# First token groups in a written order, token sets halved when made, two weight buffers, in an FNet plus ReGLU kernel

## The chip, the cores and the metric

The kernel runs on one core of a Trainium2 chip. The metric is the device time of one execution in microseconds (us): the median of 3 runs is 1048.98 us before the change (1047.89 to 1051.33). Engines are TensorE (PE, matrix products), VectorE (DVE), ScalarE (ACT), GpSimd (POOL) and SyncE (SP, which issues most loads).

## The reference

```python
# x [1, 2048, 640]; dft_seq [2048, 2048]; dft_hid [640, 640]
# W_gate, W_up [640, 1728]; W_down [1728, 640], all float32
def _A_ref(x, dft_seq_re, dft_seq_im, dft_hid_re, dft_hid_im):
    a = jnp.einsum("bsd,ed->bse", x, dft_hid_re)
    b = jnp.einsum("bsd,ed->bse", x, dft_hid_im)
    return jnp.einsum("ts,bse->bte", dft_seq_re, a) - jnp.einsum("ts,bse->bte", dft_seq_im, b)

def _B_ref(x, W_gate, W_up, W_down):
    gate = jnp.einsum("bsd,df->bsf", x, W_gate)
    up = jnp.einsum("bsd,df->bsf", x, W_up)
    gate = gate * (gate > 0)
    return jnp.einsum("bsf,fd->bsd", gate * up, W_down)

xn = _layernorm(x, axis=-1)          # (x - mean) / sqrt(var + 1e-5), no scale or shift
return x + _A_ref(xn, ...) + _B_ref(xn, ...)
```

## The kernel before

**Splitting.** Every product is made to float32 accuracy from a reduced format: an operand is split into a high part (the copy rounded to the format, on ACT) and a low part (operand minus high, on DVE), and `mm3` (L126) issues three matmuls for a block: high by high (L129), high by low of the moving operand (L130), low by high (L131). `split` (L122) makes both parts: ACT at L123, then DVE at L124. Large matrix products are made of 2 by 2 blocks in seven products instead of eight, so sums and differences of blocks have to be split too. A matmul takes 128 by 128 weights and 512 moving columns.

**Phase 1, the sequence transform (to about 411 us).** The 2048 tokens are 8 groups of 256 (`SG` = 2 tiles of 128; `NH` = 4 groups in each half). The output columns come in 4 chunks of 512. In chunks 0 and 1 the streams `B11` and `B21` go straight over groups 0 to 7 (`first_stream`, L506), chunk by chunk in turn (`B1100 B1110 B1101 B1111 ...`: name, chunk, group); after that each chunk pair runs over `T1`, `T2`, `B22`, `T3`, `T4` with four blocks each (`stream`, L593; T10 is the first block of T1). A unit of work has a load, a preparation, a run and a finish; `drive(4, 2)` (L677) issues the load of unit i, the preparation two units later and the run four units later. Raw blocks of the transform's matrix lie in the pool `raw` (6 tiles), split blocks in a ring of 3 (`cb`), so the preparation of a block waits for the third block before it on PE.

**The layer norm** runs along with the first stream. `layernorm(g)` (L236) takes statistics on DVE (`ln_stats`, L200), the root with ACT and small DVE instructions (`ln_root`, L206), centers and scales one tile on DVE and one on ACT, makes the high part on ACT and the low part on DVE (L251). Groups 0 to 3 go to `xs_early`, groups 4 to 7 to `xs_late`. Group 0 has its own written order, `first_group` (L284), in which POOL makes the lows of the first two raw blocks in four pieces of 512 columns (L291). Group 1 has `second_group` (L263). `first_products` (L474) and `second_products` (L448) give the matmuls of groups 0 and 1 in an order of their own. `keep_in_program_order` and `issue_after` are hints to the scheduling layer that sets the order on the engines; `pin` applies the first to a list.

**Token sets.** The second and third phase work on the transposed tokens. `token_sets(q, step)` (L320) makes, in six steps for each half q of the tokens, nine blocks of 128 by 1024: five plain ones or sums (`B11, B12, B21, B22, X4`) and four sums (`T1` to `T4`). It loads rows of the transposed x and of the statistics, normalizes (`make`), forms sums (`more`) on DVE and writes the float32 result to memory (`sets`). The steps for q = 1 are placed within phase 1, nine units apart: steps 2 to 5 run in chunks 1 and 2. In chunk 3, `load_set` (L661, units `K` and `A` of L727) loads each of the nine sets through a `stage` tile and splits it on ACT and DVE into its place in `xs_early` (A) or `sets_b` (K).

**Phase 2 (`gate_up`, L786, 26 units, to about 745 us).** Unit n needs the weights of column block n: `Weights(n)` loads 128 by 1280 into the one buffer of pool `z` (L748, L750), `sums` forms differences, `high` copies (L766) and `low` subtracts (L770) into `gw`. While unit n computes, the weights of n + 1 are split, and after that `Weights(n + 2)` is loaded (L822). The copy `p1` at L812 reads the first product out of PSUM. `lead_load` (L947) fetches the first block for phase 3.

**Phase 3 (`project`)** multiplies by the transform over the hidden dimension and by the down weights, and adds x.

Of the kernel before, what the change touches and what calls it, by code (L numbers as in the profile page):

```python
# [58 lines left out]
def fnet_reglu_kernel(  # L59
# [34 lines left out]
    sets = [dram_p.tile([NSET, P, W2], F32, name=f"set{q}") for q in range(2)]  # L94
# [141 lines left out]
    def layernorm(g):  # L236
# [17 lines left out]
        if g == 2:  # L254
            with tc.issue_after(high.ins), tc.issue_after(low.ins):
                st = stage()[:, :CH].rearrange("p (j d) -> p j d", j=SG)
                for j in range(SG):
                    nc.scalar.activation(st[:, j], ln_place(0)[:, j, K2], AF.Copy, scale=stat[:, 1, 0, j : j + 1])
                keep_a21(0, st)
# [3 lines left out]
    def second_group():  # L263

        xs, bs, mv = ln_tiles(1)
        js = slice(0, SG)
        nm, r = (stat[:, i, 1, js] for i in range(2))
        with tc.issue_after(late["ln"]):
            for i in ln_stats(1, xs, bs, mv, js):
                pass  # L270
            for i in ln_root(1, mv, js):
                tc.keep_in_program_order(i)
            nmr = mv[:, js, 6]
            late["ln"] = tc.keep_in_program_order(nc.vector.tensor_tensor(nmr, nm, r, op=OP.mult)).ins
            highs = [nc.scalar.activation(xn_block(1, K14, 0)[:, j], xs[:, j, K14], AF.Identity,
                                          bias=mv[:, j, 6:7], scale=stat[:, 1, 1, j : j + 1]) for j in range(SG)]
            for j in range(SG):
                nc.vector.tensor_scalar(xs[:, j], xs[:, j], mv[:, j, 0:1], stat[:, 1, 1, j : j + 1],
                                        op0=OP.subtract, op1=OP.mult)
            low = nc.vector.tensor_tensor(xn_block(1, K14, 1), xs[:, :, K14], xn_block(1, K14, 0).bitcast(F32), op=OP.subtract)  # L280
            keep_a21(1)
        late["first"] = [i.ins for i in highs + [low]]

    def first_group(b):  # L284


        pin = lambda steps: [tc.keep_in_program_order(i) for i in steps]
        xs, bs, mv = ln_tiles(0)
        part = lambda c, j: b[c][1][:, j * CH : (j + 1) * CH]
        high = lambda c, j: [nc.scalar.activation(b[c][0][:, 0, j], part(c, j), AF.Copy)]  # L290
        low = lambda c, j: [nc.gpsimd.tensor_tensor(b[c][0][:, 1, j], part(c, j), b[c][0][:, 0, j].bitcast(F32),  # L291
                                                    op=OP.subtract)]
        j0, j1 = slice(0, 1), slice(1, 2)
        d0, d14, rest, every = slice(0, P), slice(P, 3 * P), slice(P, D), slice(0, D)
# [4 lines left out]
        pin([nc.gpsimd.tensor_tensor(mv[:, 0, 6:7], stat[:, 1, 0, 0:1], stat[:, 1, 0, 0:1], op=OP.mult)])  # L299
# [12 lines left out]
        pin(ln_stats(0, xs, bs, mv, j1))  # L312
        pin(ln_root(0, mv, j1))
        pin(ln_center(0, xs, mv, 1, every, nc.scalar))
        pin(ln_scale(0, xs, 1, d0))
        pin(ln_scale(0, xs, 1, d14))
        pin(high(1, 1))
        late["ln"] = pin(low(1, 1))[-1].ins

    def token_sets(q, step, stage=stage, unit=None):  # L320
# [6 lines left out]

        def later(load, make, keep):
            def begin():
                load()  # L330
                for m in make:
                    defer(6, m)
                defer(8, keep)

            todo.append((begin, idle, idle, idle))

        unit = unit or later

        if step < 2:
# [12 lines left out]
            unit(load, [make], lambda: nc.gpsimd.dma_start(sets[q][X4][:, cs], t["a"]))  # L352
            return

        k, hs = (step - 2) // 2, (step - 2) % 2 * HC
        hs = slice(hs, hs + HC)
        cols = lambda ap: ap.rearrange("p (c t) -> p c t", c=2)

        def load():
            t["mr"], t["ab"] = stage(), stage()  # L360
            for i in range(2):
                nc.gpsimd.dma_start(cols(part(t["mr"], i)), cols(st_r[i : i + 1])[:, :, hs].to_broadcast([P, 2, HC]))
                nc.gpsimd.dma_start(cols(part(t["ab"], i)), cols(ch[k + 2 * i])[:, :, hs])

        def make():
            mr, ab = t["mr"], t["ab"]
            for i in range(2):
                tc.keep_in_program_order(tt(part(ab, i), part(ab, i), part(mr, 0), op=OP.add))
                tt(part(ab, i), part(ab, i), part(mr, 1), op=OP.mult)

        def more():

            mr, ab = t["mr"], t["ab"]
            (a0, a1, b0, b1), (t1, t2, t3, t4) = ([st[:, i * HC : (i + 1) * HC] for i in range(4)] for st in (ab, mr))
            sub = lambda o, i0, i1: tt(o, i0, i1, op=OP.subtract)
            sub(t1, a1, a0)
            sub(t2, b1, t1)
            sub(t3, b1, a1)
            sub(t4, b0, t2)

        def keep_sets():
            cs = slice(k * CH + hs.start, k * CH + hs.stop)
            for i, st in ((B11, t["ab"]), (T1, t["mr"])):
                nc.gpsimd.dma_start(sets[q][i : i + 4, :, cs].rearrange("i p t -> p i t"),
                                  st.rearrange("p (i t) -> p i t", i=4))

        unit(load, [make, more], keep_sets)
# [60 lines left out]
    def second_products(b):  # L448

        keys = [("e1", 0), ("e1", 1), "v1"]  # L450
        for js, vs in (((0,), (0, 2)), ((1,), (0, 2)), ((0, 1), (1,))):
            for j in js:
                for v in vs:
                    for d, key in zip((0, 1, 4), keys):
                        nc.tensor.matmul(E[0, key], xn_part(SG + j, d)[v == 1], b[:, int(v == 2), j], start=False, stop=False)
# [18 lines left out]
    def first_products(j, b):  # L474

        keys = [("e1", 0), ("e1", 1), "v1"]
        for v, cs in (((0, (0,)), (1, (0,)), (2, (0,)), (0, (1,)), (1, (1,)), (2, (1,))),
                      ((0, (0,)), (2, (0,)), (0, (1,)), (1, (0,)), (2, (1,)), (1, (1,))))[j]:
            for c in cs:
                for d, key in zip((0, 1, 4), keys):  # L480
                    if j == 0 and v == 0:
                        E[c, key] = bank()
                    nc.tensor.matmul(E[c, key], xn_part(j, d)[v == 1], b[c][0][:, int(v == 2), j],  # L483
                                     start=j == 0 and v == 0, stop=False)
# [21 lines left out]
    def first_stream(c, name, g):  # L506
# [7 lines left out]
        def load():  # L514
            if n == 0 and c == 0:
                st = start["raw"] = [raw(), raw()]
                for j in range(SG):
                    ln_load(0, slice(j, j + 1))
                    for k in range(2):
                        i = (k + j) % 2  # L520
                        nc.sync.dma_start(st[i][:, j * CH : (j + 1) * CH], dft[i, 0, 0][:, j * CH : (j + 1) * CH])
# [3 lines left out]
            if n > 0 or c > 1:  # L525
                t["s"] = raw()
                nc.sync.dma_start(t["s"], dft[c, 0, n])

        def prepare():
# [4 lines left out]
            if norm is not None:  # L534
                (second_group if norm == 1 else lambda: layernorm(norm))()
            if n > 0 or c > 1:
                t["b"] = b = parts()

                with ExitStack() as order:
                    for i in late["first"] if (c, n) == (1, 1) else ():  # L540
                        order.enter_context(tc.issue_after(i))
                    split(flat(b, 0), flat(b, 1), t["s"])

        def run():
# [3 lines left out]
            if n == 1 and c == 0:  # L548
                second_products(t["b"])
                return  # L550
            accs = [(c, ("e1", i)) for i in range(2)]
            product(g, t["b"], resident(n, 0), accs, half == 0, half == 1, ((c, "v1"), half, half == 0))
# [96 lines left out]

    def set_parts(q, i):  # L650
        if i in SETS_A:
            t, b = xs_early, (SETS_A_NEXT, SETS_A)[q].index(i) * 2 * W2
        else:
            t, b = late["sets_b"][q], SETS_B.index(i) * 2 * W2
# [6 lines left out]
    def load_set(q, blocks, get=stage):  # L661
        t = {}
# [12 lines left out]
        return load, prepare, idle, idle  # L675
# [21 lines left out]
    def phase(c, names):  # L697


        for n in names.split():  # L700
            if n == "K":
                todo.append(load_set(1, [first_sets.pop(0)]))
            elif n == "A":
                todo.append(load_set(1, [early_sets.pop(0)]))
# [545 lines left out]
```

## Time and profile before

| What | Value |
|---|---|
| median of 3 runs | 1048.98 us |
| span of the profiled execution, first to last instruction | 1043.3 us |
| PE busy | 1028.4 us (99%) |
| DVE busy | 802.1 us (77%) |
| ACT busy | 433.5 us (42%) |
| POOL busy | 95.7 us (9%) |
| matmuls | 4528, of which 48 warm up |
| mean granted PE clock | 0.997 |

The profile is of one execution, and of that one only the span is known, not a time of its own beside the runs; the three runs lie 4.6 to 8.0 us above the span, their median 5.7.

How to read what follows. A line of the timeline has the start, the duration, the engine, the line of the program, the operation, output <- inputs, shape and count, and in brackets the idle time of the engine just before it with what ended it. "L124 DVE cb<-raw,cb" is thus the low part of a transform block. In a list of waits stand the total, the number of times and the longest. A line of windows begins with the stretch and its length, then for each engine busy us and (xcount), then the granted clock of PE, the share of DMA engines at work and the rate in GB/s. A matmul is shown with 0.39 us but starts 0.227 us after the one before.

### The profile page before, as it was taken

The numbers are of one execution on the slowest core, as the hardware profiler recorded it, in microseconds if no ns is written. First come the engines' busy times: TensorE is split into PE (matmuls) and PEld (weight loads), VectorE is DVE, ScalarE is ACT, GpSimd is POOL, SyncE is SP. The second block draws the span as 40 slices with busy tenths as digits, with TensorE's granted clock in tenths as the row PEclk, the third lists the DMA queues.
The fourth block names the chain that finished last, engine by engine and source line by source line (L and its number), as shares of the span: only waits on it lengthen the run. The fifth ranks groups of instructions, "written<-read, shape, count | busy, mean of one in ns | idle before, by whom it ended". The sixth has DMA issues, their size and how long they took to land.

```text
span 1043.3 us, 12416 instructions
## 1 busy us (share of the span) xinstructions
PE 1028.4 (99%) x4528; PEld 847.3 (81%) x4528; DVE 802.1 (77%) x1071; ACT 433.5 (42%) x543; POOL 95.7 (9%) x156
## 2 busy tenths in 40 slices
PE   8999999999999899899999999999999999999998
PEld 7888888888887788688888888888888888888886
DVE  7857886978979887577887988887488667786764
ACT  6654453333333443333334534343355423552521
POOL 2000010101211001421110000100000000000000
PEclk9999999999999999999999999999999999999999
DMA  7985754958867863863364566565498637986454
GB/s 294 340 247 170 261 161 140 311 205 269 305 199 259 339 203 116 251 222 143 131 206 177 203 224 232 215 237 188 145 393 287 207 111 218 366 300 233 157 159 121
DMA packets 100156, 233.29 MB, mean 224 GB/s; under 512 B 11392, under 2 KB 50816, under 8 KB 98688
## 3 DMA queue, kind: packets, MB, share of 16 engines
q1 hardware_dynamic: 83664, 166.96, 47.6%
q0 software_dynamic: 16432, 65.55, 17.4%
q8 instruction: 35, 0.57, 0.2%
q14 instruction: 25, 0.20, 0.1%
HBM read 177.41 MB, written 54.02 MB: 222 GB/s over the span
## 4 chain that ended last, share of the span: by engine, by line
PE 84%; DMA 5%; DVE 5%; issue 4%; ACT 2%; POOL 0%; SPq 0%; ACTq 0%; POOLq 0%; DVEq 0%
PE ps L131 27%; PE ps L130 27%; PE ps L129 27%; DMA z<-in_wgu 2%; DVE cb L124 1%; DMA r<-in_x 1%; DMA st<-set 1%; PE ps L1147 1%; PE ps L483 1%; ACT cb L123 1%; DMA set<-st 1%; DMA rw<-hd 1%; DVE raw L595 0%; DVE gw L770 0%; ACT gw L120 0%
## 5 line engine op out<-in xcount | busy, mean ns | idle before, releaser
L131 PE MATMUL ps<-cb,wt 128*128 128x512 f32 x390 | 151.9, 390 | 0.1
L129 PE MATMUL ps<-cb,wt 128*128 128x512 f32 x390 | 151.8, 389 | 0.0
L130 PE MATMUL ps<-cb,wt 128*128 128x512 f32 x390 | 151.7, 389 | 0.0
L124 DVE TENSOR_TENSOR cb<-rw,cb 128x1024 fp32r<-128x1024 f32 x83 | 94.2, 1135 | 66.6 <-ACT cb L123 65.9
L123 ACT ACTIVATE cb<-rw 128x1024 fp32r<-128x1024 f32 x83 | 81.9, 987 | 145.2 <-PE ps L131 125.0
L123 ACT ACTIVATE cb<-raw 128x1024 fp32r<-128x1024 f32 x78 | 82.5, 1059 | 124.9 <-PE ps L131 108.3
L124 DVE TENSOR_TENSOR cb<-raw,cb 128x1024 fp32r<-128x1024 f32 x78 | 95.1, 1221 | 41.2 <-ACT cb L123 38.0
L130 PE MATMUL ps<-xs_early,gw 128*128 128x512 f32 x260 | 101.2, 389 | 0.0
L129 PE MATMUL ps<-xs_early,gw 128*128 128x512 f32 x260 | 101.2, 389 | 0.0
L131 PE MATMUL ps<-xs_early,gw 128*128 128x512 f32 x260 | 101.1, 389 | 0.0
L130 PE MATMUL ps<-cb,xs_late 128*128 128x512 f32 x256 | 99.8, 390 | 0.9 <-DVE cb L124 0.8
L131 PE MATMUL ps<-cb,xs_late 128*128 128x512 f32 x256 | 99.7, 389 | 0.3 <-DVE xs_late L251 0.3
L129 PE MATMUL ps<-cb,xs_late 128*128 128x512 f32 x256 | 99.6, 390 | 0.4 <-ACT cb L123 0.4
L130 PE MATMUL ps<-cb,xs_early 128*128 128x512 f32 x238 | 92.8, 390 | 1.5 <-DVE cb L124 1.5
L129 PE MATMUL ps<-cb,xs_early 128*128 128x512 f32 x238 | 92.6, 391 | 1.1 <-ACT cb L123 1.1
L120 ACT ACTIVATE gw<-z 128x1024 fp32r<-128x1024 f32 (+1 forms) x52 | 57.8, 1111 | 84.2 <-DVE z L760 68.7
L131 PE MATMUL ps<-cb,xs_early 128*128 128x512 f32 x238 | 92.1, 389 | 0.0
L131 PEld LDWEIGHTS ps<-cb,wt 128*128 128x128 f32 x390 | 73.2, 188 | 15.7 <-DVE wt L124 0.5
L130 PEld LDWEIGHTS ps<-cb,wt 128*128 128x128 f32 x390 | 73.2, 188 | 15.4
L129 PEld LDWEIGHTS ps<-cb,wt 128*128 128x128 f32 x390 | 73.2, 188 | 15.2
L120 ACT ACTIVATE u<-ps 128x512 f32<-128x512 f32 x52 | 31.2, 599 | 93.0 <-PE ps L131 93.0
L770 DVE TENSOR_TENSOR gw<-z,gw 128x1024 fp32r<-128x1024 f32 (+1 forms) x52 | 64.8, 1286 | 2.3 <-ACT gw L120 2.2
(192 smaller groups left out, 1932.1 us busy)
## 6 DMA issues: line engine op xcount, KB each, us to landing
raw<-in_dft SPq DMA_DIRECT2D x94, 512.0 KB, 5.7
wt<-wparts SPq DMA_DIRECT2D x66, 256.0 KB, 3.2
z<-in_wgu SPq DMA_DIRECT2D x26, 640.0 KB, 4.0
hd<-ob POOLq DMA_DIRECT2D x26, 512.0 KB, 3.5
rw<-hd SPq DMA_DIRECT2D x24, 512.0 KB, 6.1
wparts<-pw POOLq DMA_DIRECT2D x11, 1024.0 KB, 4.1
tk<-in_dft SPq DMA_DIRECT2D x16, 512.0 KB, 6.2
rw<-pq SPq DMA_DIRECT2D x16, 512.0 KB, 7.7
```

The source lines that it names most:

```text
L120: return nc.scalar.activation(o, i, AF.Copy)
L123: nc.scalar.activation(hi, src, AF.Copy)
L124: return nc.vector.tensor_tensor(lo, src, hi.bitcast(F32), op=OP.subtract)
L129: nc.tensor.matmul(ps, wh, mh, start=first, stop=False, skip_group_check=more)
L130: nc.tensor.matmul(ps, wh, ml, start=False, stop=False, skip_group_check=more)
L131: nc.tensor.matmul(ps, wl, mh, start=False, stop=last, skip_group_check=more)
L483: nc.tensor.matmul(E[c, key], xn_part(j, d)[v == 1], b[c][0][:, int(v == 2), j], start=j == 0 and v == 0, stop=False)
L770: tt(self.w[:, 1, cs], self.z[:, cs], self.w[:, 0, cs].bitcast(F32), op=OP.subtract)
L1147: nc.tensor.matmul(B[key], wr[:, v, es], hr[:, cs], start=False, stop=v == 1, skip_group_check=not new)
```

## The change

1. **Start.** `first_group` is rewritten: loads come as token tile 0, raw block of chunk 0 (first half), token tile 1, then the other raw halves; POOL's lows are placed behind a DVE result (`behind_vector`, a one-element POOL instruction that reads it), and DVE makes one of the four. `second_group` becomes `next_group`, which pins the order of groups 1 to 3; for groups 2 and 3, POOL makes the low of chunk 0's raw block in two pieces, for group 1 DVE does. `next_products` orders the matmuls of groups 1 to 3 of chunk 0, with the tokens' low part last.
2. **Token sets of q = 1.** `halve` splits each result when it is made, in one of eight places of a work area, and both halves are written to memory (`halves`, twice the bytes). In chunk 3 `load_halves` loads 128 by 2048 straight into place; its units `K` and `A` stand later in the list. Sets of q = 0 are stored whole as before, and `next_set` loads and splits them as before.
3. **Weights.** Pool `z` has two buffers; `Weights(n + 2)` is loaded at the beginning of `gate_up(n)`.
4. `lead_load` is ordered behind the last weights' load, `rest_weights` behind the last transform block.

```diff
+    def behind_vector(src):
+        src = src.bitcast(F32)
+        pin([nc.gpsimd.tensor_tensor(root_t, src, src, op=OP.mult)])
+
+    def next_group(g, b, raw, before):
+        xs, bs, mv = ln_tiles(g)
+        js = slice(0, SG)
+        nm, r = (stat[:, i, g, js] for i in range(2))
+        nmr = mv[:, js, 6]
+        low = lambda engine, j: pin([engine.tensor_tensor(flat(b, 1)[:, j], raw[:, j], flat(b, 0)[:, j].bitcast(F32), op=OP.subtract)])
+        pin(ln_stats(g, xs, bs, mv, js))
+        pin([nc.scalar.activation(flat(b, 0), raw, AF.Copy)])
+        if before is not None:
+            behind_vector(before)
+            for j in range(SG):
+                low(nc.gpsimd, slice(j * CH, (j + 1) * CH))
+        pin(ln_root(g, mv, js))
+        pin([nc.vector.tensor_tensor(nmr, nm, r, op=OP.mult)])
+        pin(nc.scalar.activation(xn_block(g, K14, 0)[:, j], xs[:, j, K14], AF.Identity,
+                                 bias=mv[:, j, 6:7], scale=stat[:, 1, g, j : j + 1]) for j in range(SG))
+        if before is None:
+            low(nc.vector, slice(0, W2))
+        pin(nc.vector.tensor_scalar(xs[:, j], xs[:, j], mv[:, j, 0:1], stat[:, 1, g, j : j + 1],
+                                    op0=OP.subtract, op1=OP.mult) for j in range(SG))
+        late["ln"] = pin([nc.vector.tensor_tensor(xn_block(g, K14, 1), xs[:, :, K14], xn_block(g, K14, 0).bitcast(F32),
+                                                  op=OP.subtract)])[0].ins
+        keep_a21(g)
...
     def first_group(b):
...
-        pin(high(0, 0))
-        pin(low(0, 0))
+        high(0, 0)
         h0, h14 = ln_scale(0, xs, 0, d0), ln_scale(0, xs, 0, d14)
         pin([next(h0)])
         pin(ln_center(0, xs, mv, 0, rest, nc.vector))
         pin([next(h14)])
-        pin(high(1, 0))
-        pin(low(1, 0))
+        high(1, 0)
         pin(h0)
         pin(h14)
-        pin(high(0, 1))
-        pin(low(0, 1))
+        behind_vector(places(0)[1][:, 3 * P - 1 : 3 * P])
+        low(0, 0, nc.gpsimd)
...
+        high(0, 1)
...
+        low(1, 0, nc.vector)
...
+        high(1, 1)
+        pin([nc.vector.tensor_tensor(l[:, K14], whole, h[:, K14].bitcast(F32), op=OP.subtract)])
+        behind_vector(l[:, 3 * P - 1 : 3 * P])
+        low(0, 1, nc.gpsimd)
+        low(1, 1, nc.gpsimd)
...
+        def begin():
+            load()
+            for i, (make, name, place, view) in enumerate(made):
+                def halve(make=make, name=name):
+                    for m in make:
+                        m()
+                    src = t[name]
+                    t["h" + name] = h = work()[:, : src.shape[1]]
+                    split(h.bitcast(F32R), src.bitcast(F32R), src)
+
+                def keep(name=name, place=place, view=view):
+                    for v, part in enumerate((t["h" + name], t[name])):
+                        nc.gpsimd.dma_start(place(v), view(part))
+
+                defer(6 + i, halve)
+                defer(8 + i, keep)
...
+    def load_halves(i):
         def load():
             if "sets_b" not in late:
                 late["sets_b"] = {1: get_r1(F32R)}
-            for i in blocks:
-                t[i] = get()
-                nc.sync.dma_start(t[i], sets[q][i])
-
-        def prepare():
-            for i in blocks:
-                split(*set_parts(q, i), t[i])
+            t, b = set_place(1, i)
+            with tc.issue_after(late["dma"]):
+                nc.sync.dma_start(t[:, b : b + 2 * W2].bitcast(F32), halves[i].rearrange("p v t -> p (v t)"))
...
-    phase(NCHUNK - 1, "T10 K T11 T12 K T13 T20 B220 K T21 B221 K T22 T23 B222 B223 T30 A T31 A T32 A T33 A T40 A T41 T42 T43")
+    phase(NCHUNK - 1, "T10 T11 T12 T13 T20 B220 T21 B221 T22 T23 K K K A A B222 B223 T30 A T31 A T32 A T33 T40 T41 T42 T43 K")
...
-    for n, b, side in (("prep", 2, "left"), ("z", 1, "left"), ("wr", 1, "left"), ("tmp", 1, "left"), ("hob", 2, "left"),
+    for n, b, side in (("prep", 2, "left"), ("tmp", 1, "left"), ("wr", 1, "left"), ("hob", 2, "left"), ("z", 2, "left"),
...
     def gate_up(n):
...
+        if n + 2 < NU:
+            weights[n + 2] = Weights(n + 2)
         for f in issues[n]:
             f()
...
-            if n + 2 < NU:
-                weights[n + 2] = Weights(n + 2)
             for f in loads[n]:
                 f()
```

More of the change, by code (lines that the diff above doesn't have):

```diff
@@ L93, in fnet_reglu_kernel @@
     rows = dram_p.tile([2, S], F32, name="rows")
-    sets = [dram_p.tile([NSET, P, W2], F32, name=f"set{q}") for q in range(2)]
+    sets = dram_p.tile([NSET, P, W2], F32, name="set0")
+    halves = dram_p.tile([NSET, P, 2, W2], F32, name="set1")
     firsts = [dram_p.tile([P, 3, CH], F32, name=f"first{c}") for c in range(NCHUNK)]
@@ L284, in first_group @@
     def first_group(b):
[L287 removed]
         xs, bs, mv = ln_tiles(0)
         part = lambda c, j: b[c][1][:, j * CH : (j + 1) * CH]
[L290 to L292 removed]
+        high = lambda c, j: pin([nc.scalar.activation(b[c][0][:, 0, j], part(c, j), AF.Copy)])
@@ L326, in token_sets @@
         t = {}
[L328 to L337, printed above, removed]
         if step < 2:
@@ L365, in make @@
[L365 to L379, printed above, removed]
@@ new lines, in token_sets @@
+        if unit:
+            unit(load, made[0][0], keep_whole)
+            return
+        def begin():
[12 more added lines that the diff above has]
+                defer(8 + i, keep)
```

192 lines of the change are left out of this document (108 added, 84 removed).

## The prediction

> **What bounds the kernel now.** I read the page first, then the waits of TensorE, then windows, then the timeline at each place where a window comes out short.
>
> ```profile
> span 1043.3 us, 12416 instructions
> PE 1028.4 (99%) x4528; PEld 847.3 (81%) x4528; DVE 802.1 (77%) x1071; ACT 433.5 (42%) x543; POOL 95.7 (9%) x156
> ```
>
> TensorE (PE) is busy 99% of the span; the change keeps its 4480 matmuls (4528 less 48 warming ones). So only the slots that PE loses can be won, and each new one costs directly. Who makes PE wait:
>
> ```profile
> PE ps L129 <- ACT p L120: 3.7, 1, 3.7
> PE ps L130 <- DVE cb L124: 2.3, 3, 0.8
> PE ps L129 <- ACT cb L123: 1.5, 2, 1.1
> PE ps L483 <- DVE xs_early L230: 1.3, 2, 0.9
> PE ps L131 <- DVE xs_late L251: 0.3, 1, 0.3
> ```
>
> Where they lie, by windows (us; the x behind PE counts matmuls, PEclk comes before the DMA share):
>
> ```profile
> 0.00:20.00 20.00, 17.35 (x91) 14.28 (x92) 14.72 (x42) 12.09 (x25) 6.38 (x10) 0.91 0.91 350
> 40.00:60.00 20.00, 19.70 (x87) 16.02 (x86) 18.67 (x44) 16.00 (x26) 1.12 (x2) 1.00 0.98 360
> 250.00:300.00 50.00, 49.87 (x220) 40.81 (x219) 43.31 (x51) 18.21 (x18) 8.96 (x14) 1.00 0.84 297
> 300.00:350.00 50.00, 47.25 (x204) 37.72 (x202) 41.24 (x46) 16.29 (x16) 5.83 (x9) 1.00 0.77 268
> 350.00:400.00 50.00, 48.96 (x215) 40.32 (x216) 45.12 (x44) 23.91 (x25) 1.07 (x2) 1.00 0.59 203
> 400.00:450.00 50.00, 46.33 (x198) 37.94 (x197) 30.30 (x48) 15.68 (x20) 17.37 (x27) 0.97 0.67 208
> 450.00:500.00 50.00, 50.00 (x222) 41.38 (x222) 40.47 (x68) 17.87 (x25) 6.53 (x10) 1.00 0.46 170
> ```
>
> ```profile
> 6.62 0.50 PE L483 MATMUL ps<-cb,xs_early 128*128 128x512 f32 x1 [0.30 <-ACT xs_early L229]
> ...
> 18.45 0.84 PE L455 MATMUL ps<-cb,xs_early 128*128 128x512 f32 x3
> ```
>
> An undisturbed window has 222 matmuls, one per 0.227 us. Missing are 18 + 7 = 25 between 300 and 400 (5.7 us), 24 between 400 and 450 (5.4 us), 2 after 250 (0.5 us), and at the start 91 - 48 = 43 are run by 20 us where (20 - 6.6)/0.227 = 59 would fit from the first one at 6.62 us: 3.6 us. These are some 15 us; the change touches all four places.
>
> **Set loads in chunk 3: -5.4 us.** ScalarE (ACT), at the first and the last of three such places:
>
> ```profile
> 333.61 1.06 ACT L123 ACTIVATE r<-st 128x1024 fp32r<-128x1024 f32 x1 [5.37 <-DMA st<-set]
> ...
> 348.23 1.06 ACT L123 ACTIVATE r<-st 128x1024 fp32r<-128x1024 f32 x1 [4.55 <-DMA st<-set]
> ```
>
> Each time ACT stands at the split of a set that has not landed, the high part of the next stream's block is queued behind it, then its low on VectorE (DVE), and PE waits for both. The change loads finished halves by DMA alone, so ACT no longer stands there, and nine splits leave both engines. Of the 5.7 us I take 5.4, since counts are good to one. The loads move past nothing on ACT, but they do on SP's queue: four A loads now wait for matmuls of T21 to T23 with the T4 blocks queued behind them (last rival).
>
> **Second weight buffer: -5.4 us.** The other large wait:
>
> ```profile
> 432.82 0.39 PE L131 MATMUL ps<-xs_early,gw 128*128 128x512 f32 x1
> 436.88 0.79 PE L129 MATMUL ps<-r,gw 128*128 128x512 f32 x1 [3.67 <-ACT p L120]
> ...
> 440.03 0.42 PE L130 MATMUL ps<-r,gw 128*128 128x512 f32 x1
> ```
>
> ```profile
> 435.29 1.06 ACT L120 ACTIVATE gw<-z 128x1024 fp32r<-128x1024 f32 x1 [6.88 <-DMA z<-in_wgu]
> ```
>
> ```profile
> 414.58 1.36 DVE L770 TENSOR_TENSOR gw<-z,gw 128x1152 fp32r<-128x1152 f32 x1 [1.24 <-ACT gw L120]
> ...
> 426.12 2.68 DVE L770 TENSOR_TENSOR gw<-z,gw 128x1024 fp32r<-128x1024 f32 x2
> ```
>
> ```profile
> DMA to landing us min/median/max: 4.2/5.9/8.4
> ```
>
> The copy p that PE waits for stands behind ACT's first copy of weights 2, whose load waited for the single buffer: free at 426.12 + 2.68 = 428.8, landed 435.3. PE loses 436.88 - 432.82 - 0.23 = 3.8 us, and then runs seven matmuls from 436.88 to 440.03 at half rate, 3.15 us instead of 1.6: 5.4 in all. With two buffers the load waits for weights 0's low instead, over at 415.9; the longest load of the last line lands by 424.3, seven us ahead of need. Loads 0 and 1 also wait for less than before; the load for the third phase goes behind the last weights, still ahead of its use.
>
> **Split when made: +2.3 and +2.0 us.** Each of steps 2 to 5 gains two ACT copies and two DVE lows, steps 0 and 1 half of one each.
>
> ```profile
> L124 DVE TENSOR_TENSOR cb<-rw,cb 128x1024 fp32r<-128x1024 f32 x83 | 94.2, 1135 | 66.6 <-ACT cb L123 65.9
> ```
>
> Two lows are 2 x 1.135 = 2.27 us of DVE. ACT has room (18.2 of 50 us in 250:300). DVE has 6.7 of 50 there, but not in the places where steps 3 and 5 fall:
>
> ```profile
> 254.30 1.23 DVE L124 TENSOR_TENSOR cb<-raw,cb 128x1024 fp32r<-128x1024 f32 x1 [0.36 <-ACT cb L123]
> ...
> 269.54 1.23 DVE L124 TENSOR_TENSOR cb<-raw,cb 128x1024 fp32r<-128x1024 f32 x1
> ```
>
> ```profile
> 270.82 0.50 PE L130 MATMUL ps<-cb,xs_late 128*128 128x512 f32 x1
> ```
>
> ```profile
> 320.00:326.00 6.00, 6.00 (x28) 4.97 (x27) 6.00 (x8) 2.20 (x3) 1.31 (x2) 1.00 1.00 285
> ```
>
> ```profile
> 325.66 2.36 DVE L124 TENSOR_TENSOR cb<-raw,cb 128x1024 fp32r<-128x1024 f32 x2
> ```
>
> ```profile
> 326.93 0.39 PE L129 MATMUL ps<-cb,xs_late 128*128 128x512 f32 x1
> 327.15 0.40 PE L130 MATMUL ps<-cb,xs_late 128*128 128x512 f32 x1
> ```
>
> Step 3: from 254.3 DVE runs without a gap to the low of T43 (269.54 to 270.77), for which PE already waits about 0.5 us. In the built order of the changed kernel the two new lows stand ahead of it on DVE, and PE's order there is unchanged: the wait grows by 2.27. Step 5: DVE is full from 320 to 326 (6.00 of 6.00), and its low for T40 is over at about 326.9, 0.3 us before PE's 327.15; the new lows stand ahead of it too, so PE waits 2.27 - 0.3 = 2.0. Steps 2 and 4 fall beside T2 blocks, where the list has no wait of PE, and 0 and 1 are halves: taken as 0, covered by DVE's lead on PE there, with 2 x 2.27 + 2 x 0.6 = 5.7 if that cover is gone. Bounds for the part: 0 (DVE finds the time behind the T lows) to 4.3 + 5.7 = 10.0.
>
> **The start: +1.0 us.** Beside GpSimd (POOL) DVE's small products are slow:
>
> ```profile
> 6.61 2.77 DVE L230 SCALAR_TENSOR_TENSOR xs_early<-r,stat,xs_early 128x128 fp32r<-128x128 f32 x2
> ...
> 12.36 0.35 DVE L230 SCALAR_TENSOR_TENSOR xs_early<-r,stat,xs_early 128x128 fp32r<-128x128 f32 x1 [0.35 <-ACT xs_early L229]
> ```
>
> ```profile
> 6.55 2.55 POOL L291 TENSOR_TENSOR cb<-raw,cb 128x512 fp32r<-128x512 f32 x2
> ```
>
> Two took 2.77 us beside POOL, one of them alone 0.35. The change lets POOL start only after them, so the 1.3 us of L483's wait goes, and with PE busy also most of the half-rate stretch (0.91 over 20 us is 1.8 us of clock). Adding the rows in the new order I have matmul 37 (first of group 1) at 16.25 instead of the 18.45 shown above: 2.2 us ahead. That lead must pass group 4:
>
> ```profile
> 41.00 1.26 ACT L120 ACTIVATE xs_late<-r 128x1280 fp32r<-128x1280 f32 x1
> ...
> 43.11 1.06 ACT L120 ACTIVATE sb<-ps 128x512 f32<-128x512 f32 x2
> ```
>
> ```profile
> 42.29 1.49 DVE L251 TENSOR_TENSOR xs_late<-r,xs_late 128x1280 fp32r<-128x1280 f32 x1
> ```
>
> Before, PE waited for that last low (0.3 in the list); DVE is 18.67 of 20 us busy there, so it paces this place, not PE. In the new order two sb copies (1.06) come ahead of ACT's high of group 4 and wait for PE's products of group 3, and one more DVE low (1.2) ahead of its low. By the rows I get the high at about 43.9 and the low at 45.4 instead of 42.3 and 43.8. PE arrives at 40.8 (43 less the lead) and goes on at 44.0 to 44.3, with seven matmuls that need highs alone; the same work stood at about 43.5 before (the low's 43.8 less the 0.3). The lead is given back, and 0.5 to 0.8 more: +0.65. Idle that long may bring the half rate of 436.88, 1.5 us; I put in a quarter, 0.35. Bounds: -2.5 (lead kept, the 0.3 gone too) to +2.2.
>
> [...]
>
> **The sum** is made against the profiled execution, whose span is 1043.3; the median 1048.98 lies 5.7 above it. 1043.3 - 5.4 - 5.4 + 2.3 + 2.0 + 1.0 = 1037.8 in the profile, and 1043.5 as a median.
>
> **Rivals.** (B) The splits hide: PE's queue at T43 and T40 is served after all. For it speaks the 13% of DVE that is free in 250:300; against it the two gapless stretches. 1043.5 - 4.3 = 1039.2. (C) The start keeps its lead, if group 4's chain runs earlier than I added up; for it speaks that POOL takes two lows of 1.2 us from DVE. 1043.5 - 1.0 - 2.5 = 1040.0. (D) The second buffer does not do what it says: the wait at 433 stays since the copy p stands behind another late load. Loads of up to 8.4 us speak for it, 7 us of room against. 1043.5 + 5.4 = 1048.9. (F) All splits go on the path, since each delay eats the reserve of the next: 10.0 instead of 4.3, 1049.2. (E) The other side, slower: the halves' loads hold up T4.
>
> ```profile
> GB/s 294 340 247 170 261 161 140 311 205 269 305 199 259 339 203 116 251 222 143 131 206 177 203 224 232 215 237 188 145 393 287 207 111 218 366 300 233 157 159 121
> ```
>
> When T23 ends, about 2.5 MB are outstanding (two A loads of 1 MB, T40's block of 0.5 MB behind them). PE reaches T40 two B22 blocks (18 matmuls each) and four T3 blocks (12 each) later: 84 x 0.227 = 19 us, of which the chain subtract, high, low takes 3.5. It decides when 2.5 MB take more than 15.5 us, below 160 GB/s. At 120 GB/s, near the lowest slices, they take 20.8: 5.3 late, and T41 to T43 (4.2 us of load against 2.7 of matmuls) 1.5 each: +9.8, 1053.3. Against it: the low slices look like low demand, as the start runs at 350.
>
> **How the numbers follow.** Forecast 0.42 (own range 1040.5 to 1047.5), B 0.21, C 0.10, D 0.10, E 0.10, F 0.07. About 0.3%, 3.1 us, can be told from no change: faster is below 1045.8, slower above 1052.1. Faster: 0.33 of the forecast, B and C, 0.64. Same: 0.08 of the forecast, 0.09 of D, 0.04 of F, 0.21. Slower: E, and 0.05 that mishaps add to the forecast, D and F, 0.15. The range of eight in ten goes from 1037.5 (B with half of C's gain) to 1050.5 (F with the start's upper bound); outside are E and the ends of B and F.
>
> **What would show it.** Right: no "ACT r<-st" with idle by DMA in 330 to 350, 222 matmuls in that window and in the one with the second phase's third unit; PE's waits for "DVE cb" at T43 and T40 grown to about 2.8 and 2.0 us; L230's successor short at 6.6; a wait of some 3 us for "xs_late" near 41. Wrong: those DVE waits missing (B); the matmul after group 4 starting by 42 (C); a wait for p left (D); waits on T4 blocks behind "DMA raw<-in_dft" (E); waits for DVE at T2 blocks too (F).

## The result and the profile after

| | before | after |
|---|---|---|
| median, us (lowest to highest, runs) | 1048.43 (1046.3 to 1051.33, 4) | 1041.05 (1040.59 to 1042.72, 4) |
| span of the profiled execution, us | 1043.3 | 1038.7 |

The ratio after to before is 0.9934, 95% interval 0.9914 to 0.9954: the changed kernel is faster, by 7.4 us between the medians, where 5.5 was forecast. The profiled executions lie only 4.6 us apart. When the same two kernels ran again later, with more executions (6 of the changed kernel beside 11), it was 5.8 us (1046.59 less 1040.80).

The list of PE's waits of the changed kernel (lines are shifted: `mm3` issues at L130 to L132, `split` is L124 and L125, `copy` L121):

```profile
PE ps L130 <- ACT xs_late L121: 2.8, 1, 2.8
PE ps L130 <- ACT cb L124: 1.8, 2, 1.4
PE ps L131 <- DVE cb L125: 1.2, 1, 1.2
...
PE ps L523 <- ACT xs_early L230: 0.9, 1, 0.9
...
PE ps L130 <- ACT wt L124: 0.4, 1, 0.4
PE ps L132 <- DVE wt L125: 0.4, 1, 0.4
```

Its windows:

```profile
40.00:60.00 20.00, 17.15 (x76) 13.87 (x75) 18.58 (x45) 13.96 (x24) 1.12 (x2) 1.00 0.95 355
...
250.00:300.00 50.00, 48.05 (x210) 38.84 (x209) 46.78 (x55) 21.06 (x21) 11.86 (x17) 1.00 0.89 307
300.00:350.00 50.00, 48.70 (x212) 39.15 (x211) 45.37 (x50) 17.81 (x17) 6.74 (x10) 1.00 0.79 296
350.00:400.00 50.00, 50.00 (x222) 41.39 (x222) 35.84 (x36) 17.12 (x17) 1.09 (x2) 1.00 0.80 309
400.00:450.00 50.00, 50.00 (x222) 41.39 (x221) 34.81 (x54) 17.47 (x23) 18.33 (x29) 1.00 0.69 222
```

The wait for p is gone, and 400 to 450 is full. So is 350 to 400. But 40 to 60 has lost 11 more matmuls (76 for 87) and 250 to 300 ten more (210 for 220), and 300 to 350 still lacks ten, eight of them in a stop at 329 to 332 us: new stops stand where the forecast put them. The timeline of PE, then ACT, at the first:

```profile
40.45 0.39 PE L132 MATMUL ps<-cb,xs_early 128*128 128x512 f32 x1
43.69 0.50 PE L130 MATMUL ps<-cb,xs_late 128*128 128x512 f32 x1 [2.85 <-ACT xs_late L121]
```

```profile
39.65 1.08 ACT L121 ACTIVATE sb<-ps 128x512 f32<-128x512 f32 x2
40.60 0.93 ACT L248 ACTIVATE r<-r,mv,stat 128x640 f32<-128x640 f32 x1
41.41 1.07 ACT L124 ACTIVATE cb<-raw 128x1024 fp32r<-128x1024 f32 x1
42.36 1.28 ACT L121 ACTIVATE xs_late<-r 128x1280 fp32r<-128x1280 f32 x1
```

The high of group 4 ends at 43.64 (43.9 was added up), PE is there at 40.7 (40.8) and goes on at 43.69 (44.0 to 44.3). At the second, the block T43, DVE makes the two new lows (`r<-r`) first, then the difference that goes into the block (L646); ACT's high of the block waits for that difference:

```profile
264.08 2.36 DVE L125 TENSOR_TENSOR r<-r 128x1024 fp32r<-128x1024 f32 x2
...
268.75 1.23 DVE L646 TENSOR_TENSOR raw<-raw,tk 128x1024 f32<-128x1024 f32 x1
```

```profile
270.09 1.06 ACT L124 ACTIVATE cb<-raw 128x1024 fp32r<-128x1024 f32 x1 [5.96 <-DVE raw L646]
```

```profile
269.40 0.39 PE L132 MATMUL ps<-cb,xs_late 128*128 128x512 f32 x1
271.20 0.73 PE L130 MATMUL ps<-cb,xs_late 128*128 128x512 f32 x2 [1.41 <-ACT cb L124]
```

So the order on DVE is behind this stop, as forecast (`steps_b22` below tests it), but PE waits first for the high of ACT and not, as forecast, for the low of DVE. At the third, the block T40, the two new lows run at 323.76, and PE waits for DVE's low:

```profile
323.76 2.36 DVE L125 TENSOR_TENSOR r<-r 128x1024 fp32r<-128x1024 f32 x2
```

```profile
331.85 0.50 PE L131 MATMUL ps<-cb,xs_late 128*128 128x512 f32 x1 [1.22 <-DVE cb L125]
```

At the very start the small products of DVE stand clear of POOL and are short, 0.35 and 0.49 us, where before two took 2.77. The first matmul of group 1 starts at 16.07 us (16.25 was added up):

```profile
16.07 4.15 PE L495 MATMUL ps<-cb,xs_early 128*128 128x512 f32 x17
```

```profile
6.39 0.35 DVE L231 SCALAR_TENSOR_TENSOR xs_early<-r,stat,xs_early 128x128 fp32r<-128x128 f32 x1
6.89 0.49 DVE L231 SCALAR_TENSOR_TENSOR xs_early<-r,stat,xs_early 128x256 fp32r<-128x256 f32 x1 [0.15 <-ACT xs_early L230]
```

### The profile page after: what moved, and what is told of

It reads as the page before. It is cut to its first block, busy times and chain, and to the rows that moved or that the text cites. A ratio compares the mean times of both kernels' runs of the same rounds, so it can differ in the third digit from the quotient of the medians.

```text
span 1038.7 us, 12463 instructions
## 1 busy us (share of the span) xinstructions
PE 1025.0 (99%) x4528; PEld 844.2 (81%) x4528; DVE 801.3 (77%) x1074; ACT 432.1 (42%) x544; POOL 106.9 (10%) x172
## 4 chain that ended last, share of the span: by engine, by line
PE 91%; DVE 5%; DMA 1%; ACT 1%; issue 1%; SPq 0%; DVEq 0%; ACTq 0%
PE ps L132 30%; PE ps L131 30%; PE ps L130 30%; DVE cb L125 1%; PE ps L1198 1%; PE ps L495 1%; DMA rw<-hd 1%; DVE raw L646 1%; DMA raw<-in_dft 1%; DVE r L125 0%; DVE tk L646 0%; ACT cb L124 0%; DVE bs L204 0%; DVE r L391 0%; DVE r L384 0%
## 5 line engine op out<-in xcount | busy, mean ns | idle before, releaser
L130 PE MATMUL ps<-cb,wt 128*128 128x512 f32 x390 | 151.9, 390 | 0.4 <-ACT wt L124 0.4
L132 PE MATMUL ps<-cb,wt 128*128 128x512 f32 x390 | 151.9, 390 | 0.4 <-DVE wt L125 0.4
L125 DVE TENSOR_TENSOR cb<-rw,cb 128x1024 fp32r<-128x1024 f32 x83 | 94.1, 1134 | 69.3 <-ACT cb L124 68.7
L124 ACT ACTIVATE cb<-rw 128x1024 fp32r<-128x1024 f32 x83 | 81.9, 987 | 149.9 <-PE ps L132 124.8
L124 ACT ACTIVATE cb<-raw 128x1024 fp32r<-128x1024 f32 x75 | 79.4, 1060 | 132.1 <-PE ps L132 101.6
L125 DVE TENSOR_TENSOR cb<-raw,cb 128x1024 fp32r<-128x1024 f32 x75 | 91.5, 1223 | 42.0 <-ACT cb L124 41.8
L130 PE MATMUL ps<-cb,xs_late 128*128 128x512 f32 x256 | 99.3, 390 | 4.3 <-ACT xs_late L121 2.8
L130 PE MATMUL ps<-xs_early,gw 128*128 128x512 f32 x260 | 101.2, 389 | 0.0
L132 PE MATMUL ps<-xs_early,gw 128*128 128x512 f32 x260 | 101.1, 389 | 0.0
L132 PE MATMUL ps<-cb,xs_late 128*128 128x512 f32 x256 | 99.3, 389 | 0.0
L121 ACT ACTIVATE gw<-z 128x1024 fp32r<-128x1024 f32 (+1 forms) x52 | 57.6, 1110 | 77.7 <-DVE z L808 75.1
L132 PE MATMUL ps<-cb,xs_early 128*128 128x512 f32 x226 | 87.9, 389 | 0.0
L131 PE MATMUL ps<-cb,xs_early 128*128 128x512 f32 x226 | 87.9, 389 | 0.0
L130 PE MATMUL ps<-cb,xs_early 128*128 128x512 f32 x226 | 87.4, 390 | 0.4 <-ACT cb L124 0.4
L130 PEld LDWEIGHTS ps<-cb,wt 128*128 128x128 f32 x390 | 73.2, 188 | 16.1 <-ACT wt L124 0.9
L132 PEld LDWEIGHTS ps<-cb,wt 128*128 128x128 f32 x390 | 73.2, 188 | 15.9 <-DVE wt L125 0.7
L121 ACT ACTIVATE u<-ps 128x512 f32<-128x512 f32 x52 | 31.1, 599 | 93.7 <-PE ps L132 93.7
```

Source lines behind the costliest of these rows:

```text
L121: return nc.scalar.activation(o, i, AF.Copy)
L124: nc.scalar.activation(hi, src, AF.Copy)
L125: return nc.vector.tensor_tensor(lo, src, hi.bitcast(F32), op=OP.subtract)
L130: nc.tensor.matmul(ps, wh, mh, start=first, stop=False, skip_group_check=more)
L131: nc.tensor.matmul(ps, wh, ml, start=False, stop=False, skip_group_check=more)
L132: nc.tensor.matmul(ps, wl, mh, start=False, stop=last, skip_group_check=more)
```

## The experiments

All were run beside the kernel before in three groups of four, in the order of the table, with 4 to 12 executions of each kernel. The kernel before has a median of 1046.67, 1046.59 and 1047.31 us in them (23, 11 and 17 executions). In every execution, of any kernel, the time lies 1.7 to 2.1 us above the span of that same execution.

| kernel | median, us | ratio to before | 95% interval | profiled span |
|---|---|---|---|---|
| z_one | 1042.15 | 0.9946 | 0.9925 to 0.9967 | 1039.5 |
| sets_old | 1042.66 | 0.9959 | 0.9945 to 0.9974 | 1041.1 |
| start_old | 1038.81 | 0.9919 | 0.9899 to 0.9939 | 1038.6 |
| pools | 1043.30 | 0.9972 | 0.9957 to 0.9988 | 1041.3 |
| same_after | 1040.80 | 0.9947 | 0.9926 to 0.9968 | 1039.6 |
| lead_old | 1040.32 | 0.9943 | 0.9923 to 0.9964 | 1037.6 |
| steps_b22 | 1036.68 | 0.9899 | 0.9882 to 0.9916 | 1033.5 |
| g4_first | 1039.46 | 0.9928 | 0.9913 to 0.9943 | 1037.6 |
| weights_old | 1047.54 | 1.0004 | 0.9991 to 1.0016 | 1044.7 |
| weights_only | 1039.63 | 0.9928 | 0.9913 to 0.9943 | 1036.0 |
| steps_g4 | 1033.11 | 0.9874 | 0.9856 to 0.9892 | 1030.6 |
| steps_start | 1033.28 | 0.9868 | 0.9851 to 0.9885 | 1031.8 |

### The weights: z_one, pools, lead_old, weights_old, weights_only

`z_one`, one buffer again:

```diff
-    for n, b, side in (... ("hob", 2, "left"), ("z", 2, "left"),
+    for n, b, side in (... ("hob", 2, "left"), ("z", 1, "left"),
...
-        if n + 2 < NU:
-            weights[n + 2] = Weights(n + 2)
         for f in issues[n]:
...
                 ahead.low(1)
+            if n + 2 < NU:
+                weights[n + 2] = Weights(n + 2)
```

> The changed kernel with one weight buffer again and the load of weights n + 2 behind the split of n + 1. Theory (the wait for p was the single buffer's): PE stops once near 430 us for some 4 us on p, 3.8 us lost, 5.4 if a half-rate stretch follows; the first loads of the third phase find their memory free an earlier unit, so the stop at 754 us (1.7 us) shrinks to 0.4. Span 1041.2 to 1042.8 against 1038.7. Rival (the load was late for other reasons, and the second buffer is not what removed the wait): no stop near 430, span 1037.4 to 1039.

The stop did not come back. From its list of waits, and SP's and ACT's timelines:

```profile
PE ps L130 <- ACT p L121: 0.4, 2, 0.2
```

```profile
399.90 36.41 SPq L798 DMA_DIRECT2D z<-in_wgu  x4
```

```profile
431.25 1.06 ACT L121 ACTIVATE gw<-z 128x1024 fp32r<-128x1024 f32 x1 [3.44 <-DMA z<-in_wgu]
```

The third load still is what ACT waits for, but at 431.25, not 435.29, since the first was issued at 399.9 instead of 405.1, and each load of a single buffer follows from the one before. Two short waits on p are left. The second buffer by itself is worth about 1.0 us here (gaps of 0.62 and 0.57 us between matmuls at 432 and 445, against 0.23, and a slower matmul behind each). Theory and rival were both wrong on the span, 1039.5, and the stop at 754 us did not shrink (1.6 us lost).

`pools`, the two buffers placed last in memory:

```diff
-    for n, b, side in (... ("hob", 2, "left"), ("z", 2, "left"),
-                       ("stage3", 2, "left"), ("sets", 1, "left"), ("gw1", 1, "right")):
+    for n, b, side in (... ("hob", 2, "left"), ("stage3", 2, "left"),
+                       ("sets", 1, "left"), ("z", 2, "left"), ("gw1", 1, "right")):
```

> The changed kernel with the weight buffers placed last among the second phase's pools, so that the first loads of the third phase do not lie over the memory of the sets, whose last matmul is near 733 us; nothing else differs. Theory (a late start of these loads bunches them with the hidden-state loads): they are issued some 12 us earlier, the stop at 754 us falls from 1.7 to 0.4 us or less, span about 1037.4. Rival (those loads are late since the transfers are slow there anyway): 1038.7.

It was made for the third phase (below), but it bears on this one too: with the buffers in the new place the first load goes out 10 us later. That the new place lies over memory which phase 1 holds longer is the likely reason; it was not shown.

```profile
409.88 27.62 SPq L798 DMA_DIRECT2D z<-in_wgu  x5
```

Yet PE has no stop over 0.3 us between 425 and 450. So a late first load with two buffers does no harm there, and one buffer with an early first load does little. `lead_old` takes the changed place of `lead_load` alone back:

```diff
-        with tc.issue_after(weights[NU - 1].ins):
-            nc.sync.dma_start(r, pqd[2][0][:, :2])
-            nc.sync.dma_start(s, ...)
+        nc.sync.dma_start(r, pqd[2][0][:, :2])
+        nc.sync.dma_start(s, ...)
```

> The changed kernel with the first load for the third phase free to move forward again; two weight buffers stay. Theory (the wait for p near 430 us needed both, a first weight load held up in the queue by that load and a single buffer; either remedy alone is enough): the first weight load is issued some 4 us later than in the changed kernel, and PE still has no stop of over 1 us between 425 and 450. Rival (the earlier first load alone removed it): a stop of 3 us or more on p.

There is no stop, but for another reason than the theory gave: the first weight load still left at 400.0, as the order on SP put the second half of that load, at 403.3, behind it. So this edit alone does not make the first load late. `weights_old` takes all of it back: `z_one`'s edit, `lead_old`'s, the order of the pools (`z` before `wr`), and `rest_weights`. Which of the last three makes the first load late there was not separated; the order of the pools can, as `pools` shows.

> The changed kernel with all that concerns the second phase's weights as before: one buffer, loads of n + 2 behind the split of n + 1, the order of the pools in memory, the first load for the third phase free to move forward. Theory (the stop on p needs a late first load and a single buffer together): the first weight load is issued 4 us or more later than in the changed kernel, and PE stops near 430 us for 3.5 us or more; with the half rate behind it the span is 1042.5 to 1044.5. Rival (the stop came from loads that the set loads of chunk 3 delayed, and is gone with those): no stop over 1 us there, span 1038 to 1039.5.

```profile
PE ps L130 <- ACT p L121: 4.3, 1, 4.3
```

```profile
404.71 36.33 SPq L798 DMA_DIRECT2D z<-in_wgu  x4
```

```profile
435.98 1.06 ACT L121 ACTIVATE gw<-z 128x1024 fp32r<-128x1024 f32 x1 [7.45 <-DMA z<-in_wgu]
```

The stop is back, 4.3 us, with a half-rate stretch behind it; the span, 1044.7, is 0.2 above the expected range:

```profile
437.00:441.00 4.00, 3.42 (x9) 2.77 (x10) 4.00 (x7) 2.77 (x5) 1.16 (x2) 0.65 0.58 205
```

With it goes the whole gain: the ratio is 1.0004 (interval 0.9991 to 1.0016) with start and token sets still as changed. `weights_only` is the counterpart, start and sets as before:

> The kernel before with the change's weights part alone (start and token sets as before). Theory (the parts add up): the stop near 433 us is gone (5.4 us), all else is as before, span between 1037 and 1040, and the time some 5 us under that of the kernel before. Rival (a part of the gain needs the other parts): less than 3 us.

```profile
300.00:350.00 50.00, 46.61 (x201) 37.15 (x200) 41.57 (x47) 17.48 (x17) 3.75 (x6) 1.00 0.72 258
400.00:450.00 50.00, 50.00 (x222) 41.41 (x221) 34.94 (x54) 16.19 (x22) 18.72 (x29) 1.00 0.65 205
```

300 to 350 still lacks 21 matmuls, 400 to 450 is full, and the time is 7.7 us under that of the kernel before in its group (1047.31): as much as the whole change (the span, 1036.0, is 1 us under the expected range). The other two parts together are worth nothing that can be told from noise.

### The token sets: sets_old, steps_b22

`sets_old` stores the sets of q = 1 whole and splits them in chunk 3:

```diff
-                nc.sync.dma_start(t[:, b : b + 2 * W2].bitcast(F32), halves[i].rearrange("p v t -> p (v t)"))
+                nc.sync.dma_start(t[i], sets[q][i])
...
+            for i in blocks:
+                split(*set_parts(q, i), t[i])
...
-    phase(NCHUNK - 1, "T10 T11 T12 T13 T20 B220 T21 B221 T22 T23 K K K A A B222 ... T43 K")
+    phase(NCHUNK - 1, "T10 K T11 T12 K T13 T20 B220 K T21 B221 K T22 T23 B222 ... A T41 T42 T43")
```

> The changed kernel with the token sets of q = 1 stored whole again, and loaded and split in chunk 3 as before. Theory: the three stops behind ACT r<-st return (5.3 us lost), the stops at T43 (2.8 us) and T40 (1.8 us) fall back to 0.5 and 0: net +1.2, span about 1039.9. Rival (the waits at T43 and T40 come from the start's and the loads' shift, not from the two added lows): they stay, span about 1044.

```profile
333.44 1.06 ACT L123 ACTIVATE r<-st 128x1024 fp32r<-128x1024 f32 x1 [5.07 <-DMA st<-set]
...
348.43 1.06 ACT L123 ACTIVATE r<-st 128x1024 fp32r<-128x1024 f32 x1 [5.50 <-DMA st<-set]
```

The three stops return, and those at T43 and T40 fall to 0.5 us and none; behind the last stop matmuls run at half rate until 355.7 (seven 0.43 us apart, clock 0.57 from 352 to 356), which the expectation did not have: 1041.1 for 1039.9. In the medians the halves are worth some 1 to 2.5 us (1042.66 against 1040.80 and 1041.05, the ratio 0.9959 against 0.9947 and 0.9934), but the intervals of these ratios overlap, so the medians alone do not show it. `steps_b22` keeps the halves and moves the steps:

```diff
-            if n == "V3":
-                free[0] = len(todo) + 2
-            if free[0] is not None and len(todo) >= free[0] and steps:
-                token_sets(*steps.pop(0))
-                free[0] = len(todo) + SPACE
+            if steps and n in (("T21", "B222"), ("T12", "T21"), ("T12", "T21"), ())[c]:
+                token_sets(*steps.pop(0))
```

> The changed kernel with the six token-set steps of q = 1 begun so that their arithmetic and splits fall beside the T2 and B22 blocks (two steps in each of chunks 0, 1 and 2), instead of every nine units. Theory (DVE's lows of the splits stand ahead of the lows of T43 and T40): the stops at 269 to 273 us (2.8 us) and 329 to 332 us (1.8 us) go down to 0.3 or less each, no new stop beside T2 and B22; span down by 4.2 to about 1034.5. Rival (DVE is full there without them): stops of over 1.5 us stay, or come up beside T2.

```profile
200.00:250.00 50.00, 50.00 (x223) 41.40 (x222) 44.97 (x51) 20.08 (x21) 7.78 (x11) 1.00 0.64 235
250.00:300.00 50.00, 50.00 (x222) 41.44 (x221) 44.94 (x51) 19.97 (x20) 9.64 (x14) 1.00 0.84 318
300.00:350.00 50.00, 50.00 (x222) 41.40 (x222) 45.23 (x49) 17.91 (x17) 5.95 (x9) 1.00 0.83 314
```

All three windows are full, with DVE as busy as in the changed kernel (135 of 150 us, and 134 there). The work was not too much for DVE; it stood at the wrong place. The span fell by 5.2 against the 4.2 expected; 0.3 of the rest is a gap of 0.45 us between matmuls at 340 us, which is gone too.

### The start: start_old, g4_first, same_after

`start_old` has `first_group`, `second_group` and their products as before.

> The changed kernel with the start of before (first_group, second_group, products). Theory (the lead of the start is given back at group 4, and 0.4 more): PE's stop of 3.0 us at 40 us becomes 0.5, the waits for L230 and half-rate matmuls at 8 to 13 us return, span 1038.3. Rival (the written order is what wins): span 1040.5 to 1041.

```profile
PE ps L506 <- ACT xs_early L230: 1.4, 1, 1.4
...
PE ps L506 <- DVE xs_early L231: 0.9, 1, 0.9
```

```profile
40.00:60.00 20.00, 20.00 (x90) 16.57 (x89) 18.67 (x44) 16.14 (x26) 1.12 (x2) 1.00 0.99 370
```

The waits at the start return, 40 to 60 is full, and the time is the lower of the two: its six executions span 1035.8 to 1038.6, the median 1036.9, those of the changed kernel (`after` and `same_after`, ten) 1037.6 to 1042.7, the median 1039.1. By these the new start costs 2.2 us, and not 0.4 as the theory had it. The profiled one, 1038.6, had the longest span of the six. `same_after` is the changed kernel unaltered:

> The changed kernel again, unaltered, beside the others of this group. Theory (executions differ by half-rate stretches of some 1.7 us each after PE's longer stops): the span lies between 1038.5 and 1042, and where it is over 1040 the timeline has matmuls 0.43 us apart behind the stop at 40 us. Rival (the first profile was typical): 1038.7 within 0.5, no such stretch.

The same 3.2 us stop at 40 us, and here with half-rate matmuls behind it:

```profile
43.70:46.50 2.80, 2.80 (x7) 2.22 (x8) 2.63 (x9) 0.98 (x5) 0.55 (x1) 0.50 0.99 411
```

The span, 1039.6, is within the theory's range, but the half rate is there below 1040 us already, and the six executions span 1037.6 to 1042.7. Eight profiles of this study have this stop (waits of 2.8 to 2.9 us); two (`same_after`, and `pools` with a clock of 0.55 from 43.7 to 47.1) have the half rate behind it. `g4_first` changes the order around group 4:

```diff
+        if g == NH:
+            late["high4"], late["low4"] = high.ins, low.ins
...
-                    if c == 1 and n < NH:
+                    if c == 1 and n < NH or (c, n) == (0, NH):
                         order.enter_context(tc.issue_after(late["ln"]))
+                    if (c, n) == (1, NH):
+                        order.enter_context(tc.issue_after(late["low4"]))
...
+                    if c == 1 and not half:
+                        order.enter_context(tc.issue_after(late["high4"]))
                     copy(s[:, i], E[c, key])
```

> The changed kernel with the layer norm of group 4 put ahead: its roots before the two lows of chunk 0's and 1's block 4 on DVE, its high part ahead of the three sb copies and the next block's high on ACT. Theory (ACT's and DVE's order, not the data, holds group 4 back): PE's stop at 40 us falls from 3.0 to 0.5 us or less, span down by 2.5. Rival (the statistics come too late, whatever the order): the stop stays over 2 us.

```profile
42.04 0.50 PE L130 MATMUL ps<-cb,xs_late 128*128 128x512 f32 x1 [1.15 <-ACT xs_late L121]
```

```profile
39.76 0.93 ACT L248 ACTIVATE r<-r,mv,stat 128x640 f32<-128x640 f32 x1
40.72 1.27 ACT L121 ACTIVATE xs_late<-r 128x1280 fp32r<-128x1280 f32 x1
```

The order was more than half of it: the high ends at 41.99 instead of 43.64, and PE loses 1.3 us, not 3.0. What is left is the chain itself, with the low of one transform block (L125) still ahead of L246, the first step of the layer norm's scaling, on DVE. The span of the profile gains only 1.1 of the 2.5 expected, as a half-rate stretch of eight matmuls fell at 271 behind the T43 stop (clock 0.55 from 271 to 274).

### Together: steps_g4, steps_start

> The changed kernel with the token-set steps beside T2 and B22 and with group 4's layer norm put ahead. Theory (the two stops have nothing to do with each other): the gains add, 1033.5 less 1.3 to 1.7, span 1032, and no half-rate matmuls after the shorter stop. Rival (what one wins the other loses): span 1033.5 or more.

> The changed kernel with the token-set steps beside T2 and B22 and with the start of before. Theory (the written order of the start wins nothing, since its lead is lost at group 4): no stop at 40 us, two waits and half-rate matmuls between 6 and 14 us, span 1032 to 1034 and a time not above that of the steps with the changed start. Rival (the written start is worth its 2.2 us): span 1035.5 or more.

Both add up, and both beat both kernels: 1033.1 and 1033.3 us, 14 us under the kernel before. Their spans, 1030.6 and 1031.8, are a little under what was expected. The two cannot be told apart (the intervals overlap). Beside `steps_b22`, which has the new start and group 4 as changed, `steps_start` is 3.4 us lower between the medians (the intervals just overlap): a second sign that the new start, with group 4 left as it is, costs time. The list of PE's waits of `steps_g4` has 1.2 us at group 4 as its longest entry.

## Why the prediction was right

By the time alone the forecast does not stand out: 1041.05 lies near the lower end of its own range, 1040.5 to 1047.5, and nearer to rival C (1040.0) than to 1043.5. What speaks for the forecast is the traces, part by part.

**Second weight buffer (-5.4).** Right in place and near in size: 6.6 us in `weights_old`'s profile (4.4 of idle at the wait for p, 1.7 of half rate behind it, 0.5 at smaller gaps) and 6 to 8 us in the medians. It was incomplete in what it credited: the prediction had the wait end because the load no longer waits for the single buffer. The runs show two remedies in this part, the second buffer and a first load that goes out 5 us earlier, and either alone leaves 1.0 us or less. The prediction passed over the second one in its sentence that loads 0 and 1 wait for less.

**Set loads (-5.4) and splits (+2.3, +2.0).** Right, with one link different. The three stops at the set loads lost 5.3 us before; a gap of 0.3 near there is left after, so 4.9 were won. In the profile after, the stops at 269 to 273 us come to 2.8 us, 2.3 more than before, and those at 329 to 332 to 1.8. At T43 the two lows delay the difference and through it ACT's high, where the prediction had PE wait for DVE's low. The net gain agrees with what `sets_old` loses, 1 to 2.5 us, as far as that can be told. Rivals B and F are out: the lows were not hidden, and only two of six steps cost PE more than 0.4 us.

**The start (+1.0).** The mechanism was right: a lead won and given back at group 4. By the 151st matmul (the warming ones counted) PE is 2.2 us ahead (31.16 us against 33.41); by the 351st, behind group 4, it is 0.3 us late (79.65 against 79.33). So this pair of profiles shows +0.3, but one pair is too few. In the four profiles with the old start the 351st matmul begins at 78.1 to 79.6 us, on average at 78.9; in the eight with the new start and group 4 as changed at 79.5 to 81.3, on average at 80.0. That is 1.2 us, of which the half rate behind the 3.2 us stop, in two of the eight, makes 0.4 and the rest 0.8; the prediction had 0.35 (a chance of one in four) and 0.65. The other 1.0 of the 2.2 us between the median spans was not traced to a place. Behind that stop the profiles differ: in the profile after, matmuls that start 3.24 us apart (40.45 and 43.69) are followed by the full rate (0.23 us apart, clock 1.00 from 40 to 46 us), and behind the same stop in `same_after` and `pools` (waits of 2.9 and 2.8 us) the clock is 0.50 from 43.7 to 46.5 and 0.55 from 43.7 to 47.1. Whether the small products of DVE for groups 2 and 3 take longer beside POOL too, as the two of 2.77 us did, was hardly tested: of the root's products of these groups only one began while POOL was at work, and POOL ended its second block 0.1 us later. It took 0.16 us, as the same product of group 3 did at 30.33 us, with POOL's blocks over at 30.05.

```profile
19.82 2.54 POOL L272 TENSOR_TENSOR cb<-raw,cb 128x512 fp32r<-128x512 f32 x2
```

```profile
22.25 0.16 DVE L216 SCALAR_TENSOR_TENSOR mv<-mv 128x2 f32<-128x2 f32 x1
```

**The step that failed: how a span stands to the median.** The prediction added 5.7 us to its 1037.8, as if every execution took 5.7 us more than its span. It takes 1.8 to 2.0 us more (the medians of the two kernels). The rest of the 5.7 was chance: the kernel before spans 1041.8 to 1049.4 us over the 51 executions of the three groups, median 1044.9, so the profiled one, 1043.3, lay 1.6 below it, and the three runs behind 1048.98 lay 2.3 above it. By the right sum, 1037.8 + 1.9 = 1039.7; 1041.05 was measured. The executions of one kernel differ with the granted clock: of the 51, the 18 at 0.993 or less span 1046.5 on average, the 15 at 0.996 or more 1044.0. The changed kernel's ten are at 0.995 or more. That fewer and shorter stops leave less to the half rate would explain it, but this was not shown.

**What the sum lacked.** At the beginning of the third phase PE loses 1.7 us in the profile after (the waits for wt), 0.4 before. With it the stages of the two profiles add up to the 4.6 us between their spans: 0.3 + 2.3 + 1.8 - 4.9 - 5.4 + 1.3. `pools` issued those loads some 9 us earlier and had 0.5, but `lead_old` and `g4_first`, which do not alter them, had 0.6 and 0.8: a stop that differs between executions, its cause left open. Open too is why `pools` is 2 us slower than the changed kernel; its profile shows one stop of 1.6 us at 462, where ACT waits for the store of `ob`.

**The rivals.** C fell with the stop at 40 us, D with the wait gone, E with 350 to 400 full: the halves' loads held up nothing.

## What to carry to other kernels

A stop that a late load causes can have two causes in a row (here a late first issue, and a single buffer that passes lateness on); undo each alone before crediting one. When an engine as busy as DVE here (44.9 to 46.8 of 50 us between 250 and 350 in the changed kernel and `steps_b22`) takes on more work, the place of that work in its order can decide, and not the sum: here the same lows cost 4 us ahead of a critical one and nothing beside longer blocks. A sum made on one profiled execution is not better than the spread between executions, here 7 us for one kernel: set a predicted span against measured spans, not against a median of three runs. A lead won at the start is kept only if the next place that another engine paces comes earlier too.

## What the hardware showed that was not expected

Executions of one unaltered kernel differ by up to 7 us in span (1041.8 to 1048.9 in one group of 23), at granted clocks of 0.991 to 0.997. Half-rate stretches come behind the stop at 40 us (3.2 us) in two of eight profiles (clock 0.50 in `same_after`, 0.55 in `pools`) and not in the other six: the mean clock of the whole execution is 1.000 in the profile after, `z_one` and `steps_b22` and 0.999 in `lead_old`; `sets_old` and `weights_old`, at 0.998, have a stretch elsewhere, at 352 and 437 us. In `g4_first` one also comes behind two stops close together, with matmuls 1.80 and 0.80 us apart (271 to 274 us, clock 0.55); the same two stops in the profile after have none behind them (clock 1.00).
